# Row counts of a split DRAM write, and the place of a sign factor, in an FFT filter followed by a cosine-gated feed-forward

## The chip, the cores and the metric

The kernel runs on one core of a Trainium2 chip. The core has five engines that run side by side, each through its own list of instructions in order: TensorE (PE: matmuls; its weight loads are the separate row PEld), VectorE (DVE), ScalarE (ACT), GpSimd (POOL) and SyncE (SP), which here only issues DMA transfers. ScalarE issues transfers too. All transfers go through sixteen DMA engines. The metric is the device time of one execution in microseconds (us), the median of several runs.

## The reference

```python
def _attn_ref(x, filt_r, filt_i):            # x: (8, 3008, 256); filters: (1505, 256)
    X = np.fft.rfft(x, axis=1)
    F = (filt_r + 1j * filt_i)[None, :, :]
    return np.fft.irfft(X * F, n=x.shape[1], axis=1).astype(np.float32)

def _moe_ref(x, w_in, w_out):                # x: (24064, 256); w_in: (256, 2048); w_out: (2048, 256)
    h = x @ w_in
    g = h * np.cos(h)
    return (g @ w_out).astype(np.float32)
```

The second function is applied to the first one's result, with batch and sequence taken together. Everything is float32.

## The kernel before

**Arithmetic.** A float32 matmul of full accuracy is made of three faster ones: an operand is cut into a high part (a cast) and a low part (the rest), and `mm3` (L249) adds high x high, low matrix x high and high matrix x low. In the profile a cast to fp32r on ScalarE or VectorE is such a high part, and a TENSOR_TENSOR with subtraction, mostly on GpSimd, the low part.

**The filter** is a Fourier transform of length 3008 = 47 x 64 in four stages per batch. Stage 1 (L270) transforms over 47 and writes to DRAM (z1). `stage23` (L301) loads z1 in 12 pieces of 128 x 512 (zf), transforms over 64, multiplies by the filter, transforms back over 64 and writes to DRAM (z2). Stage 4 (L418) loads units of z2, transforms over 47 and makes the high and low part of y, the input of the feed-forward. A unit is up to five columns of the 64; there are 104, and the first three (5 + 5 + 1 columns, n_first = 3) feed the first chunk.

**The product with the filter** in `stage23`: the 128 rows of ps are 64 real parts and 64 imaginary parts. fat and fbt hold the filter's real and imaginary part, each twice, over the rows. ScalarE copies ps with its halves swapped into sw (L319, L320), VectorE multiplies ps by fat (L322), and sw by a sign per row and by fbt, in two halves of 256 columns, since each half has its own column of signs in sg (L325); then it adds the two (L327). sg holds minus the sign in its first 64 rows and plus the sign in the others. Before the next transform ScalarE makes the high part (L330) and GpSimd the low part (L331).

**The first batch** goes another way, at the start, with plain float32 matmuls: `first1` (stage 1), `first23` (L383; its z2t tiles are written to z2 here) and the first three units of stage 4. Each of the 12 tiles of `first23` has 128 rows: a column of the 64 has two of them. The write is cut in two after n0 rows: ScalarE's queue issues the first piece (L409), which the first three units need, and SP's queue the second (L412), later. n0 is 2 x 11 = 22, so the second piece has 106 rows of 2 KB.

**The feed-forward** has 47 chunks of 512 tokens, each in 8 steps: `hidden` (L458) makes a tile hp of 128 x 1024 in PSUM with 12 matmuls, `gate` (L473) makes g = h cos h with three VectorE steps (L476, L477, L479) and a Sin on ScalarE (L478) and cuts it into gh (L481, ScalarE) and gl (L483, GpSimd), and `project` (L486) adds it with 12 matmuls into two accumulators. There are two hp tiles; one is free again after L479. The weights w_in and w_out come as 64-bit floats in 16 tiles of 512 KB and are turned into high and low parts on the chip by `prep_w` (L214): the load (L222), two ScalarE steps (L231, L233), a shift on VectorE (L234), and GpSimd and ScalarE steps.

**Order.** The program fixes the order by a planner: `run_due` (L586) inserts the filter's steps for batches 1 to 7 and stage 4 between the matmuls of the feed-forward, by due times in slots. A scheduler that simulates the engines then sets the final order of each engine's list. On SP the beginning is written out by hand (L525 to L558): loads for the first batch, weights as listed in a string, then matrices. Transfers wait on eight shared completion counters, and each engine, SP too, stands at an instruction whose wait isn't over.

Of the kernel before, what the change touches and what calls it, by code (L numbers as in the profile page):

```python
# [13 lines left out]
AF = mybir.ActivationFunctionType  # L14
ALU = mybir.AluOpType

B, S, D, DFF = 8, 3008, 256, 2048
# [4 lines left out]
P = 128  # L22
# [116 lines left out]
def _units():  # L139


    sizes = [5, 5, 1] + [5] * 99 + [3, 3]
    assert sum(sizes) == B * NB
    starts = np.concatenate([[0], np.cumsum(sizes)])
    return [(int(a), int(n)) for a, n in zip(starts, sizes)]
# [10 lines left out]
def fft_filter_then_cos_glu(ctx: ExitStack, tc: tile.TileContext, ins, outT):  # L156
    nc = tc.nc
# [33 lines left out]
    sg = const.tile([P, NK], F32, name="sg")  # L191
# [6 lines left out]
    units = _units()  # L198
# [4 lines left out]
    n_first = len(of_chunk[0])  # L203

    @contextmanager
    def behind():

        if hold:
            with tc.issue_after(hold[0]):
                yield  # L210
        else:
            yield
# [36 lines left out]
    def mm3(out, m, hi, lo):  # L249

        nc.tensor.matmul(out, m[0], hi, start=True, stop=False)  # L251
        nc.tensor.matmul(out, m[1], hi, start=False, stop=False)  # L252
        nc.tensor.matmul(out, m[0], lo, start=False, stop=True)  # L253
# [7 lines left out]
    def psum_f(b):  # L261
        if b == 0 and len(done) < n_first:
            if not spare:
                spare.extend(ps_h.tile([P, 2, 512], F32, name="hp")[:, u] for u in range(2))
                spare.append(ps_f.tile([P, 512], F32, name="ps", tag="ps"))
            return spare.pop(0)
        return ps_f.tile([P, 512], F32, name="ps", tag="ps")
# [33 lines left out]
    def stage23(b, i):  # L301
        piece = slice(i * 512, (i + 1) * 512)
        f = fft.tile([P, 2, 512], F32, name="f", bufs=3)
        fbt, fat = f[:, 0], f[:, 1]
        with behind():
            nc.sync.dma_start(fbt, fb[:, piece])
            nc.sync.dma_start(fat, fa[:, piece])
        zf = fft.tile([P, 512], F32, name="zf", tag="ld", bufs=5)
        assert len(wrote1[b]) == 2 * n1
        nc.sync.dma_start(zf, z1s[b].rearrange("c (n k) d -> (c n) (k d)", k=NK)[:, piece])  # L310
        hi = fft.tile([P, 512], F32R, name="zh", tag="sh", bufs=3)
        lo = fft.tile([P, 512], F32R, name="zl", tag="sl", bufs=3)
        nc.vector.tensor_copy(hi, zf)  # L313
        nc.gpsimd.tensor_tensor(lo, zf, hi.bitcast(F32), ALU.subtract)  # L314
        yield
        ps = psum_f(b)
        mm3(ps, mats["m2"], hi, lo)
        sw = fft.tile([P, 512], F32, name="sw", bufs=2)
        nc.scalar.copy(sw[:64], ps[64:])  # L319
        nc.scalar.copy(sw[64:], ps[:64])  # L320
        ya = fft.tile([P, 512], F32, name="ya", bufs=2)
        nc.vector.tensor_tensor(ya, ps, fat, ALU.mult)  # L322
        for k in range(2):
            ks = slice(k * D, (k + 1) * D)
            nc.vector.scalar_tensor_tensor(sw[:, ks], sw[:, ks], sg[:, 2 * i + k : 2 * i + k + 1], fbt[:, ks],  # L325
                                           ALU.mult, ALU.mult)
        nc.vector.tensor_tensor(ya, ya, sw, ALU.add)  # L327
        yh = fft.tile([P, 512], F32R, name="yh", bufs=2)
        yl = fft.tile([P, 512], F32R, name="yl", bufs=2)
        nc.scalar.copy(yh, ya)  # L330
        nc.gpsimd.tensor_tensor(yl, ya, yh.bitcast(F32), ALU.subtract)  # L331
        yield
        ps = psum_f(b)
        if i == 0:
            mm3(ps[:, :D], mats["m30"], yh[:, :D], yl[:, :D])
            mm3(ps[:, D:], mats["m3"], yh[:, D:], yl[:, D:])
        else:
            mm3(ps, mats["m3"], yh, yl)
        z = fft.tile([P, 512], F32, name="z2t", tag="st", bufs=4)
        nc.scalar.copy(z, ps)  # L340
        wrote2.setdefault(b, []).append(i)
        nc.scalar.dma_start(z2[b * NJ : (b + 1) * NJ].rearrange("j (h c k) d -> (j h c) (k d)", h=2, c=2)[:, piece], z)
# [40 lines left out]
    def first23(i, fas, fbs):  # L383
        cols = slice(512 * i, 512 * i + 512)
        zf = fft.tile([P, 512], F32, name="zf", tag="ld", bufs=5)
        nc.sync.dma_start(zf, z1s[0].rearrange("j (h c k) d -> (j h c) (k d)", h=2, c=2)[:, cols])
        yield
        ps = psum_f(0)
        nc.tensor.matmul(ps, mats["f2"], zf, start=True, stop=True)
        half = slice(2 * (i % 2), 2 * (i % 2) + 2)  # L390
        ya = fft.tile([P, 512], F32, name="ya", bufs=2)
        yb = fft.tile([P, 512], F32, name="yb", tag="sw", bufs=2)
        for y, f in ((ya, fas), (yb, fbs)):
            nc.vector.tensor_tensor(y, ps, f[i // 2][:, half].rearrange("p k d -> p (k d)"), ALU.mult)
        yield
        ps = psum_f(0)
        if i == 0:
            for m, c in (("30", slice(0, D)), ("3", slice(D, 512))):
                nc.tensor.matmul(ps[:, c], mats["f" + m], ya[:, c], start=True, stop=False)
                nc.tensor.matmul(ps[:, c], mats["f" + m + "i"], yb[:, c], start=False, stop=True)  # L400
        else:
            nc.tensor.matmul(ps, mats["f3"], ya, start=True, stop=False)
            nc.tensor.matmul(ps, mats["f3i"], yb, start=False, stop=True)
        tag, bufs = at2[i]
        z = fft.tile([P, 512], F32, name="z2t", tag=tag, bufs=bufs)
        nc.scalar.copy(z, ps)
        to = z2[:NJ].rearrange("j (h c k) d -> (j h c) (k d)", h=2, c=2)[:, cols]
        n0 = 2 * units[n_first][0]
        nc.scalar.dma_start(to[:n0], z[:n0])  # L409
        yield  # L410
        wrote2.setdefault(0, []).append(i)
        nc.sync.dma_start(to[n0:], z[n0:])  # L412
# [112 lines left out]
    with tc.tile_pool(name="first", bufs=12) as first, tc.manual_schedule(engines={mybir.EngineType.SP}):  # L525
        fas, fbs, load, sign = filters(first)
        ones = [first1(i, first) for i in range(NJ // 4)]
        twos = [first23(i, fas, fbs) for i in range(n23)]
        for g in ones:
            next(g)  # L530
# [74 lines left out]
    for b in range(1, B):  # L605
        end = slot(b * S) - BEFORE
        if b == 1:
            end += LATER
        start = max(end - LENGTH, FIRST)
        step = (end - start - GAP12) / (2 * n1 + 2 * n23)  # L610
        for i in range(n1):
            t = start + step * (2 * i + 1)
            plan(stage1(b, i), t - AHEAD1, [t, t + step])
        for i in range(n23):
            t = start + step * (2 * n1 + 2 * i + 2) + GAP12
            plan(stage23(b, i), t - AHEAD2, [t, t + GAP23], lambda b=b: len(wrote1.get(b, ())) == 2 * n1)
# [73 lines left out]
```

## Time and profile before

| | |
|---|---|
| median of 3 runs | 2562.18 us (2557.64 to 2562.96) |
| the profiled execution | 2562.1 us |
| its span | 2560.3 us |
| mean granted TensorE clock | 0.979 |
| TensorE matmul busy | 2455.7 us (96%) |
| VectorE busy | 1885.4 us (74%) |
| ScalarE busy | 1286.1 us (50%) |
| GpSimd busy | 1430.5 us (56%) |
| DMA moved | 212.27 MB |
| TensorE idle, largest cause | 63.8 us in 15 waits for VectorE L479 |

Busy time is the time in which an engine has an instruction running. A share near 100% is a bound only in the stretch for which it is read: the table's 96% is a mean over a start in which TensorE often waits and a long rest. DMA-issuing instructions (SPq, ACTq) are not busy time; their length is the time that the issuing queue stood at them. "Granted clock" is the share of TensorE's full clock that the throttle let through.

### The profile page before, as it was taken

To read this page: it belongs to the slowest core of one execution; us is meant where nothing else is said; L and a number is where in the kernel's file an instruction comes from. 1 tells how busy PE (TensorE), PEld (TensorE's weight loads), DVE (VectorE), ACT (ScalarE), POOL (GpSimd) and SP (SyncE) were. 2 spreads that over 40 slices of the span, in tenths; PEclk is the share of its full clock that TensorE was granted. 3 is DMA by queue.
4 is the path that set the end of the run, shared out by engine and by line. 5 is a ranking of instruction groups with operands and counts; after the bars stand their busy time and mean duration, and the time that the engine had idled before them with its cause. 6 is when DMAs were issued, how large, how long until landed. Compare 5 with 4: busy or idle time off the path is not lost.

```text
span 2560.3 us, 29873 instructions
## 1 busy us (share of the span) xinstructions
PE 2455.7 (96%) x10783; PEld 1967.7 (77%) x10783; DVE 1885.4 (74%) x1911; ACT 1286.1 (50%) x1707; POOL 1430.5 (56%) x826
## 2 busy tenths in 40 slices
PE   7369889999999999999999999999999999999999
PEld 2257767888888888888888888888888888888887
DVE  2177987888678877888668886787768886666665
ACT  1355564555545555555545555455554554444443
POOL 1366664656656565656546665566555554444443
PEclk8679999999999999999999999999999999999999
DMA  9253342322322232222313223222312211000000
GB/s 318 72 166 89 129 144 65 119 82 82 85 83 91 90 91 71 93 90 78 93 47 105 86 85 85 79 94 74 100 43 88 99 54 48 24 21 9 17 9 17
DMA packets 134749, 212.27 MB, mean 83 GB/s; under 512 B 12521, under 2 KB 64281, under 8 KB 134601
## 3 DMA queue, kind: packets, MB, share of 16 engines
q1 hardware_dynamic: 82385, 137.97, 17.7%
q10 hardware_dynamic: 52216, 72.39, 8.8%
q8 instruction: 86, 1.41, 0.2%
q14 instruction: 62, 0.51, 0.1%
HBM read 135.33 MB, written 74.97 MB: 82 GB/s over the span
## 4 chain that ended last, share of the span: by engine, by line
PE 82%; DVE 7%; DMA 3%; issue 3%; SPq 2%; ACT 2%; POOL 1%; POOLq 0%; ACTq 0%; DVEq 0%
PE hp L466 36%; PE acc L495 36%; PE ps L435 3%; PE ps L251 2%; PE ps L252 2%; PE ps L253 2%; SPq L412 2%; DVE g L476 1%; DMA xf<-in_x 1%; DVE sw L325 1%; DVE g L477 1%; DMA raw<-in_w_in 1%; ACT g L478 1%; DVE g L479 1%; DVE xo L280 1%
## 5 line engine op out<-in xcount | busy, mean ns | idle before, releaser
L483 POOL TENSOR_TENSOR gl<-g,gh 128x1024 fp32r<-128x1024 f32 x376 | 910.7, 2422 | 825.6 <-ACT gh L481 510.7
L466 PE MATMUL hp<-y,w_in 128*128 128x512 f32 x4512 | 1132.6, 400 | 65.8 <-DVE g L479 63.8
L466 PEld LDWEIGHTS hp<-y,w_in 128*128 128x128 f32 x4512 | 845.3, 190 | 266.6 <-issue 59.8
L495 PE MATMUL acc<-gh,w_out 128*128 128x512 f32 x3008 | 896.9, 396 | 0.7 <-ACT gh L481 0.7
L479 DVE TENSOR_TENSOR g<-g,hp 128x1024 f32<-128x1024 f32 x376 | 457.9, 1218 | 320.6 <-ACT g L478 320.1
L478 ACT ACTIVATE g<-g,half_pi 128x1024 f32<-128x1024 f32 x376 | 433.4, 1153 | 484.2 <-DVE g L477 436.6
L495 PEld LDWEIGHTS acc<-gh,w_out 128*128 128x128 f32 x3008 | 564.0, 188 | 131.1 <-ACT gh L481 1.1
L481 ACT CAST gh<-g 128x1024 fp32r<-128x1024 f32 x376 | 394.9, 1051 | 430.5 <-DVE g L479 424.1
L476 DVE TENSOR_SCALAR g<-hp 128x1024 f32<-128x1024 f32 x376 | 458.8, 1220 | 137.7 <-PE hp L466 130.3
L495 PE MATMUL acc<-gl,w_out 128*128 128x512 f32 x1504 | 549.9, 400 | 1.3 <-POOL gl L483 1.3
L477 DVE SCALAR_TENSOR_TENSOR g<-g,hp 128x1024 f32<-128x1024 f32 x376 | 458.0, 1218 | 9.9
L495 PEld LDWEIGHTS acc<-gl,w_out 128*128 128x128 f32 x1504 | 283.7, 189 | 66.7 <-POOL gl L483 2.1
L452 POOL TENSOR_TENSOR y<-y,y 128x470 fp32r<-128x470 f32 (+29 forms) x142 | 124.9, 884 | 55.8 <-ACT y L449 55.8
L435 PEld LDWEIGHTS ps<-m,z 120*128 120x128 f32 (+1 forms) x816 | 129.3, 192 | 21.0
L314 POOL TENSOR_TENSOR zl<-zf,zh 128x512 fp32r<-128x512 f32 x84 | 111.7, 1330 | 47.8 <-DVE zh L313 24.5
L331 POOL TENSOR_TENSOR yl<-ya,yh 128x512 fp32r<-128x512 f32 x84 | 113.2, 1348 | 42.1 <-ACT yh L330 42.0
L435 PE MATMUL ps<-m,z 120*128 120x120 f32 (+1 forms) x816 | 129.2, 273 | 0.0
L325 DVE SCALAR_TENSOR_TENSOR sw<-sw,sg,f 128x256 f32<-128x256 f32 x168 | 116.9, 735 | 0.0
L313 DVE CAST zh<-zf 128x512 fp32r<-128x512 f32 x84 | 93.1, 1108 | 23.1 <-DMA zf<-z 13.4
L327 DVE TENSOR_TENSOR ya<-ya,sw 128x512 f32<-128x512 f32 x84 | 98.5, 1173 | 0.0
L330 ACT CAST yh<-ya 128x512 fp32r<-128x512 f32 x84 | 51.8, 618 | 91.0 <-DVE ya L327 90.7
L449 ACT CAST y<-y 128x470 fp32r<-128x470 f32 (+29 forms) x150 | 66.9, 456 | 41.3 <-DVE y L443 38.9
(96 smaller groups left out, 1413.3 us busy)
## 6 DMA issues: line engine op xcount, KB each, us to landing
z<-z SPq DMA_DIRECT2D x101, 240.0 KB
out_t<-o ACTq DMA_DIRECT2D x94, 256.0 KB
f<-in_fb SPq DMA_DIRECT2D x84, 256.0 KB
f<-in_fa SPq DMA_DIRECT2D x84, 256.0 KB
zf<-z SPq DMA_DIRECT2D x84, 256.0 KB
z<-z2t ACTq DMA_DIRECT2D x84, 256.0 KB
xf<-in_x SPq DMA_DIRECT2D x42, 480.0 KB
z<-z1t ACTq DMA_DIRECT2D x84, 240.0 KB
```

Source lines behind the costliest of these rows:

```text
L325: nc.vector.scalar_tensor_tensor(sw[:, ks], sw[:, ks], sg[:, 2 * i + k : 2 * i + k + 1], fbt[:, ks], ALU.mult, ALU.mult)
L331: nc.gpsimd.tensor_tensor(yl, ya, yh.bitcast(F32), ALU.subtract)
L435: nc.tensor.matmul(v[:, t, a * r : (a + 1) * r], zf[:, a, t * P : (t + 1) * P], mats[f"m4{a}"][:r, :r], start=True, stop=True)
L452: (nc.vector if i < 2 * n_first else nc.gpsimd).tensor_tensor(yl, part, yh.bitcast(F32), ALU.subtract)
L466: nc.tensor.matmul(hp[:, u], w_in[s][w][:, t, fs], y[:, t], start=(t == 0 and n == 0), stop=(t == NDT - 1 and n == 2))
L476: nc.vector.tensor_scalar(g, h, 0.25, MAGIC, ALU.add, ALU.add)
L477: nc.vector.scalar_tensor_tensor(g, g, MAGIC, h, ALU.subtract, ALU.subtract)
L478: nc.scalar.activation(g, g, AF.Sin, bias=half_pi, scale=-TWO_PI)
L479: nc.vector.tensor_tensor(g, g, h, ALU.mult)
L481: nc.scalar.copy(gh, g)
L483: nc.gpsimd.tensor_tensor(gl, g, gh.bitcast(F32), ALU.subtract)
L495: nc.tensor.matmul(acc, w_out[s][w][:, u, es], g[:, u], start=(s == 0 and u == 0 and n == 0), stop=(s == NFT // 2 - 1 and u == 1 and n == 2))
```

## The change

It does two things. In `first23` the write of a tile is cut after 32 rows instead of after 22: the first piece (ScalarE's queue) has 32 rows and the second (SP's queue) 96. The rows written, in sum, are the same. In `stage23` ScalarE's swapped copy becomes four activations of 64 x 256 (function Identity) that multiply by the sign as they copy, with the sign of the rows they read; VectorE then multiplies sw by fbt in one piece of 128 x 512 and subtracts where it added, since the rows read have the opposite sign of the rows written.

```diff
@@ -316,15 +316,14 @@
         ps = psum_f(b)
         mm3(ps, mats["m2"], hi, lo)
         sw = fft.tile([P, 512], F32, name="sw", bufs=2)
-        nc.scalar.copy(sw[:64], ps[64:])
-        nc.scalar.copy(sw[64:], ps[:64])
+        for k in range(2):
+            ks = slice(k * D, (k + 1) * D)
+            for to, of in ((slice(0, 64), slice(64, P)), (slice(64, P), slice(0, 64))):
+                nc.scalar.activation(sw[to, ks], ps[of, ks], AF.Identity, scale=sg[of, 2 * i + k : 2 * i + k + 1])
         ya = fft.tile([P, 512], F32, name="ya", bufs=2)
         nc.vector.tensor_tensor(ya, ps, fat, ALU.mult)
-        for k in range(2):
-            ks = slice(k * D, (k + 1) * D)
-            nc.vector.scalar_tensor_tensor(sw[:, ks], sw[:, ks], sg[:, 2 * i + k : 2 * i + k + 1], fbt[:, ks],
-                                           ALU.mult, ALU.mult)
-        nc.vector.tensor_tensor(ya, ya, sw, ALU.add)
+        nc.vector.tensor_tensor(sw, sw, fbt, ALU.mult)
+        nc.vector.tensor_tensor(ya, ya, sw, ALU.subtract)
         yh = fft.tile([P, 512], F32R, name="yh", bufs=2)
         yl = fft.tile([P, 512], F32R, name="yl", bufs=2)
         nc.scalar.copy(yh, ya)
@@ -405,7 +404,7 @@
         z = fft.tile([P, 512], F32, name="z2t", tag=tag, bufs=bufs)
         nc.scalar.copy(z, ps)
         to = z2[:NJ].rearrange("j (h c k) d -> (j h c) (k d)", h=2, c=2)[:, cols]
-        n0 = 2 * units[n_first][0]
+        n0 = 32
         nc.scalar.dma_start(to[:n0], z[:n0])
         yield
         wrote2.setdefault(0, []).append(i)
```

Lines from L327 of the old program on have numbers lower by one in the new one, so its second write is L411 and its load of a unit L424. The scheduler sets the lists of all engines anew. Two places of them:

SP's list, at the end of the twelve second pieces of the first batch's writes. z2t is the tile written, raw_684, raw_695 and raw_751 are the weights w_out, w_in and w_out of the fifth and sixth step, f the filter pieces of batch 1, z4_619 and z4_624 the loads of stage 4's units 3 and 4. Before:

```order
L412 DMA z2_112<-z2t_526 106x512
L222 DMA raw_684<-in_w_out 128x2x512
L306 DMA f_1529<-in_fb 128x512
L307 DMA f_1529<-in_fa 128x512
L306 DMA f_1593<-in_fb 128x512
L307 DMA f_1593<-in_fa 128x512
L306 DMA f_1648<-in_fb 128x512
L222 DMA raw_695<-in_w_in 128x2x512
L307 DMA f_1648<-in_fa 128x512
L222 DMA raw_751<-in_w_out 128x2x512
L425 DMA z4_619<-z2_112 120x2x256
L425 DMA z4_624<-z2_112 120x2x256
```

Here both units' loads stand behind the three weights and three pairs of filter pieces. SP's list at the same place, in the change:

```order
L411 DMA z2_112<-z2t_526 96x512
L424 DMA z4_619<-z2_112 120x2x256
L222 DMA raw_684<-in_w_out 128x2x512
L306 DMA f_1529<-in_fb 128x512
L307 DMA f_1529<-in_fa 128x512
L306 DMA f_1593<-in_fb 128x512
L307 DMA f_1593<-in_fa 128x512
L222 DMA raw_695<-in_w_in 128x2x512
L306 DMA f_1648<-in_fb 128x512
L222 DMA raw_751<-in_w_out 128x2x512
L424 DMA z4_624<-z2_112 120x2x256
```

Unit 3's load has moved up to stand right behind the writes, the second w_in (raw_695) has moved up by one, and one filter load (f_1648 of in_fa) has moved down behind what is shown.

TensorE's list, around the third hidden tile of the first chunk (hp_706). z4_619 and z4_624 are again units 3 and 4, y0 and y1 the high and low part of the first chunk, m40 and m41 stage 4's matrices. Before, the end of that tile:

```order
L466 MATMUL hp_706<-y0_554,w_in0_2_84 128x512
L466 MATMUL hp_706<-y1_555,w_in0_2_84 128x512
L466 MATMUL hp_706<-y0_554,w_in1_2_85 128x512
L435 MATMUL ps_621<-m40_310,z4_619 128x120
L435 MATMUL ps_621<-m41_312,z4_619 128x120
```

The two units' eight matmuls come after all twelve of the tile. TensorE's list in the change, the beginning of that tile:

```order
L434 MATMUL ps_657<-m41_312,z4_624 128x120
L434 MATMUL ps_657<-m40_310,z4_624 128x120
L465 MATMUL hp_706<-y0_554,w_in0_2_84 128x512
L465 MATMUL hp_706<-y1_555,w_in0_2_84 128x512
L465 MATMUL hp_706<-y0_554,w_in1_2_85 128x512
```

Unit 3's four matmuls and three of unit 4's now stand ahead of the tile.

## The prediction

> **What bounds the kernel now.** I read the waits of TensorE first, then its timeline, then followed the longest wait back through VectorE, ScalarE and SP's queue. A wait's row is engine, line, what it waited for: us in total, times, longest; a timeline row is start, length, instructions, and in brackets the idle time before it and its releaser.
>
> ```profile
> PE hp L466 <- DVE g L479: 63.8, 15, 48.2
> ...
> PE ps L251 <- DVE ya L322: 4.8, 3, 2.2
> ...
> PE hp L466 <- ACT y L449: 2.0, 1, 2.0
> ...
> PE acc L495 <- ACT gh L481: 0.7, 1, 0.7
> ...
> 400.00:2200.00 1800.00, 1798.65 (x8088) 1464.04 (x8087) 1401.64 (x1430) 955.52 (x1268) 1058.13 (x615) 1.00 0.26 81
> ```
>
> The last row is a window: its length, then busy time of PE, PEld, DVE, ACT and POOL, the granted clock, the DMA share and GB/s. From 400 us on TensorE never stands still, at a granted clock of 1.00; DVE is busy 78% there and ACT 53%. So an edit inside that stretch is worth nothing, and what is worth something is the first 400 us, where one single wait takes 48.2 us. Its chain, backwards:
>
> ```profile
> 143.80 4.58 PE L466 MATMUL hp<-y,w_in 128*128 128x512 f32 x12 [48.24 <-DVE g L479]
> ...
> 137.32 0.43 DVE L234 TENSOR_SCALAR t<-o 128x512 int32<-128x512 int32 x1 [46.97 <-ACT o L231]
> ...
> 136.55 0.66 ACT L231 ACTIVATE o<-raw 128x512 f32<-128x512 f32 x1 [44.14 <-DMA raw<-in_w_out]
> ...
> 122.52 4.30 SPq L222 DMA_DIRECT2D raw<-in_w_out  x1
> ...
> 79.06 43.36 SPq L412 DMA_DIRECT2D z<-z2t  x12
> ...
> 78.62 0.40 SPq L222 DMA_DIRECT2D raw<-in_w_in  x1
> ```
>
> TensorE wants a hidden tile back that VectorE frees (L479). VectorE stands in order behind L234, a step of the conversion of the fifth w_out tile; that waits for ScalarE, that for the raw weights, and their load was issued only at 122.52 because SP spent 43.36 us on the twelve writes of line 412. Those are slow in the engines that carry them:
>
> ```profile
> z<-z2t SPq DMA_DIRECT2D x12, 212.0 KB
> ...
> 84.00:126.00 42.00, 9.59 (x31) 7.41 (x30) 3.27 (x10) 4.58 (x10) 6.58 (x5) 0.58 0.13 51
> ...
> 1.19 11.82 SPq L373 DMA_DIRECT2D xf<-in_x  x16
> ...
> xf<-in_x SPq DMA_DIRECT2D x23, 192.0 KB
> ...
> 2.00:13.00 11.00, 9.03 (x14) 3.26 (x15) 1.67 (x3) 1.96 (x5) 0.00 (x0) 1.00 0.99 277
> ```
>
> While the 106-row writes run alone, the 16 DMA engines are busy 0.13 of the time at 51 GB/s: 0.13 x 16 is two engines. 217,088 bytes at 51 GB/s are 4.26 us each, 51 us for twelve. The 96-row loads of line 373 at the start (same row of 2 KB, 192 KB each) keep the share at 0.99 and move 277 GB/s; sixteen of them cost SP 11.82 us, 0.74 each.
>
> By the Trainium skill, page "DMA: Bandwidth & Descriptors", section "Why a DMA increments its semaphore by 16 and not by 1", a transfer uses the largest number of engines up to 16 that divides its slowest dimension. By that rule 106 rows get 2, 96 and 32 rows 16, and the 0.13 and the 0.99 agree with it. No row here is a 96-row write by itself; if the rule is taken to hold for writes too, the third rival below loses its chance of 0.05 to the forecast, whose time stays.
>
> **Part one, the first batch's writes.**
>
> ```profile
> L409 ACTq DMA_DIRECT2D z<-z2t x12: 287/288/537, 41.8 to 75.1; - x12
> ...
> z<-z2t ACTq DMA_DIRECT2D x12, 44.0 KB
> ...
> 76.63 1.28 SPq L425 DMA_DIRECT2D z<-z  x3
> ```
>
> SP's second pieces have 96 rows now, 196,608 bytes. Priced by line 373's rows, twelve take 12 x 0.74 = 8.9 us of SP where they took 43.36. ScalarE's twelve first pieces (L409) grow from 44 to 64 KB; 20 KB more at 277 GB/s are 0.07 us each, and they are issued between the weight conversions, up to 75 us. I cost them at nothing; if the last one landed later, the stage-4 loads at 76.63 would be late by that 0.07.
>
> In SP's list, shown above with the change, unit 3 (rows 22 to 31 of the tiles) now needs only the first pieces, so its load moved up past nine transfers; unit 4 still needs the twelve second pieces and follows the same loads as before. In TensorE's list the matmuls of both units moved ahead of the third hidden tile (hp_706), the one that stood 48 us.
>
> So TensorE restarts when two things are there, the freed hidden tile and unit 4's load, and I time both.
>
> ```profile
> f<-in_fb SPq DMA_DIRECT2D x84, 256.0 KB
> ...
> raw<-in_w_in SPq DMA_DIRECT2D x8, 512.0 KB
> ...
> z<-z SPq DMA_DIRECT2D x101, 240.0 KB
> ...
> 1.19 2.65 DMA xf<-in_x
> ...
> 141.74 10.22 DMA raw<-in_w_in
> ...
> 131.50:149.50 18.00, 5.70 (x24) 4.84 (x25) 8.59 (x10) 8.93 (x12) 6.56 (x5) 0.56 0.90 273
> ...
> 126.86 1.16 SPq L306 DMA_DIRECT2D f<-in_fb  x1
> ...
> 152.05 0.68 ACT L231 ACTIVATE o<-raw 128x512 f32<-128x512 f32 x1 [3.90 <-DMA raw<-in_w_in]
> ...
> 154.08 0.34 SPq L278 DMA_DIRECT2D xf<-in_x  x1
> ...
> 152.82 1.44 DVE L234 TENSOR_SCALAR t<-o 128x512 int32<-128x512 int32 x1 [2.43 <-POOL gl L483]
> ```
>
> *Hidden tile.* SP: 79.06 + 8.9 = 88.0, unit 3's load 0.4, so the weights go out at 88.4. From issue to use, 192 KB took 2.65 us on an empty queue; 320 KB more at 277 GB/s add 1.2, so 3.8 is the low end. The high end is 10.2, the weights at 141.74 behind a full queue. Ahead of ours stand only one 240 KB load and the rest of the writes, so I take 3.8: data at 92.2 instead of 136.55. From there to TensorE it was 143.80 - 136.55 = 7.25 us: 99.5 (up to 105.9).
>
> *Unit 4.* Behind raw_684 go five filter loads of 256 KB, two weights of 512 KB and unit 4's 240 KB, about 2.6 MB; at 273 GB/s, which the window around the same mix of transfers shows, 9.5 us from about 91 (the SP time for nine issues, at 0.4 to the 1.16 seen, lies inside it), plus about 1 us until its first three matmuls are through: 101.5. With the weights late by the 6.4 above it would be 108.
>
> The later one counts: 101.5 instead of 143.8, **42.3 us**, with 36 and 44.3 as ends.
>
> What is late next: the following weights landed at 151.96, 8.2 us after the restart, and ScalarE had waited 3.90 us for them and VectorE 2.43, partly because two of the sixteen engines were still draining the old writes. In the new order they go out right behind unit 4's group with an even queue, so I take the 2.4 of VectorE back; the ends are 0 and 3.9.
>
> **Part two, the filter product in batches 1 to 7** (84 pieces). What it removes and adds, by rows (line, engine, shape, count; busy, mean ns; idle before and why):
>
> ```profile
> L319 ACT COPY sw<-ps 64x512 f32<-64x512 f32 x84 | 49.1, 584 | 10.1 <-PE ps L253 8.3
> ...
> L320 ACT COPY sw<-ps 64x512 f32<-64x512 f32 x84 | 48.7, 579 | 1.0
> ...
> L295 ACT COPY z1t<-ps 96x256 f32<-96x256 f32 x14 | 4.9, 357 | 3.1 <-PE ps L253 3.1
> ...
> L478 ACT ACTIVATE g<-g,half_pi 128x1024 f32<-128x1024 f32 x376 | 433.4, 1153 | 484.2 <-DVE g L477 436.6 <-POOL gl L483 22.7 <-POOL yl L331 10.1
> ...
> L481 ACT CAST gh<-g 128x1024 fp32r<-128x1024 f32 x376 | 394.9, 1051 | 430.5 <-DVE g L479 424.1
> ...
> L325 DVE SCALAR_TENSOR_TENSOR sw<-sw,sg,f 128x256 f32<-128x256 f32 x168 | 116.9, 735 | 0.0
> ...
> L327 DVE TENSOR_TENSOR ya<-ya,sw 128x512 f32<-128x512 f32 x84 | 98.5, 1173 | 0.0
> ...
> 143.80:400.00 256.20, 234.10 (x993) 184.23 (x994) 217.79 (x219) 141.38 (x209) 173.46 (x104) 0.95 0.41 123
> ```
>
> VectorE: two products of 735 ns become one 128x512 product of two SBUF operands, for which L327 is the same form: 2 x 735 - 1173 = 0.30 us less per piece (nothing, if it were as slow as both old ones). ScalarE: two copies of 584 and 579 ns, together 1.16, become four activations of 256 columns. A plain copy of 256 columns took 357 ns; an activation with a vector operand took 1153 - 1051 = 102 ns more than a cast of the same shape. That gives 4 x 0.46 = 1.84, 0.68 us more; with no extra for the operand it is 0.27, with two such extras 1.08.
>
> The Trainium skill, page "ScalarE: Activation LUTs", section "What ACT_TABLE_LOAD costs", gives 186 ns plus 0.833 ns a column, and 93 ns for each vector operand. By it four pieces are about 1.97 us, an estimate, 0.8 more than the two copies' rows; the end at the loss side of this part, 8 us below, would be 12 x 0.8 = 9.6 by it, and the sum the same.
>
> Where does this lie? Batch 1's twelve pieces fall into the stretch up to 400 us, where VectorE is busy 218 of 256 us and a few short waits of TensorE depend on it (4.8 us for L322 in all); the other 72 lie under a full TensorE. So VectorE's gain is at most 12 x 0.30 = 3.6 us and ScalarE's longer step, if it delayed VectorE each time, at most 12 x 0.68 = 8.2 lost; the two go against each other with neither shown to be on the path each time, and I count **nothing**, from 4 gained to 8 lost. The cover in the later batches is ScalarE's slack (53% busy) and 0.7 us of waits for its gh; without it 72 x 0.68 = 49 us would appear.
>
> **Sum**, against the profiled execution, which took 2562.1 us with a span of 2560.3 (the median of the runs is 2562.18, so the same): 2562.1 - 42.3 - 2.4 + 0 = 2517.4, **2517 us**. The likeliest case alone runs from the ends 44.3 + 3.9 + 4 = 52 to 36 - 8 = 28 saved, which would need every end at once; 2509 to 2528 is what I hold for it.
>
> **Rivals.**
> 1. *The queue takes the wait over* (0.15). From 78.62 to unit 4's load 6.8 MB are issued (twelve writes and the loads counted above), 25 us at 273 GB/s; if weights, filters, unit 4 and stage 1's x all arrive at the late ends, 36 us are left and the 2.4 become a loss of about 3: 33 saved, 2529 us. For it: DMA share 0.90 already around 140 us. Against: the x loads came after 154 us.
> 2. *The short waits go too* (0.13). After the restart TensorE lost 15.6 us more to L479 (63.8 - 48.2) and 4.8 to L322, behind a VectorE filled with late weights. If half of it goes with the even queue and the lighter product, 44 + 10 = 54 us: 2508.
> 3. *It doesn't do what it says* (0.05): SP's time goes by rows, not by engines. Then 96 rows cost 43.36 x 96/106 = 39.3, 4.1 us saved: 2558. Line 373's 0.74 us speaks against it.
> 4. *Slower* (0.04): ScalarE's four pieces stand ahead of the Sin and the cast of a gate in its order; each late gate holds a hidden tile, and TensorE waits. It needs over 45 / 84 = 0.53 us of TensorE per piece in all seven batches to undo the gain; at 1.08 it would be 91 - 45 = 46 us slower, 2563 at the point of balance and 2608 at worst, 2580 in the middle. Against it: TensorE waited for ScalarE's y and gh 2.7 us in the whole run.
>
> The main case keeps 0.63. The range takes in rivals 1 and 2: **2505 to 2534**. A measurement of this kernel tells 0.2%, 5 us, from no change; faster 0.92 (the main case, rivals 1 and 2, and a bit of the other two), same 0.04, slower 0.04.
>
> **What would show it.** Right: line 411's twelve issues on SP take about 9 us; the fifth w_out weights reach ScalarE near 92 us; TensorE's wait of 48 us shrinks to about 6 and its releaser is L478 or unit 4's load; the DMA share around 85 us is near 1; the window from 400 us on is as full as before; the four activations take about 0.46 us each. Wrong: 3 us or more per write (rival 3), waits of TensorE for DMA between 100 and 150 us (rival 1), or waits for gh or L477 in the later batches (rival 4).

## The result, and the profile after

| | before | after |
|---|---|---|
| median | 2561.7 us | 2525.9 us |
| profiled execution, its span | 2562.1, 2560.3 us | 2526.6, 2524.8 us |
| restart of TensorE after the long wait | 143.80 us | 103.39 us |
| from there to the end of the span | 2416.5 us | 2421.4 us |
| VectorE, ScalarE busy | 1885.4, 1286.1 us | 1869.2, 1345.3 us |

The ratio of after to before is 0.9862 (95% interval 0.9845 to 0.9879), 36 us less. The forecast was 2517 us with a range of 2505 to 2534. The third and fourth rows already divide the result: the restart came 40.4 us earlier, and 4.9 us were lost again between the restart and the end. One of the six executions of part one alone, further down, took 4029 us at a granted clock of 0.56 and is left out of its ratio.

The timelines of SP, ScalarE and TensorE of the changed kernel, with the rows that answer to the chain shown of before (start, length, instructions; in brackets the idle time before and its releaser):

```profile
79.34 8.62 SPq L411 DMA_DIRECT2D z<-z2t  x12
88.79 0.79 SPq L222 DMA_DIRECT2D raw<-in_w_out  x1
94.45 2.32 SPq L424 DMA_DIRECT2D z<-z  x4
```

```profile
94.47 0.68 ACT L231 ACTIVATE o<-raw 128x512 f32<-128x512 f32 x1 [0.76 <-DMA raw<-in_w_out]
```

```profile
102.09 1.64 PE L434 MATMUL ps<-m,z 120*128 120x120 f32 x6 [4.01 <-DMA z<-z]
103.39 1.63 PE L465 MATMUL hp<-y,w_in 128*128 128x512 f32 x3
...
134.38 7.42 PE L465 MATMUL hp<-y,w_in 128*128 128x512 f32 x24 [2.06 <-DVE g L478]
...
153.32 7.95 PE L465 MATMUL hp<-y,w_in 128*128 128x512 f32 x21 [4.55 <-DVE g L478]
```

The twelve writes take SP 8.62 us instead of 43.36, the fifth w_out weights reach ScalarE at 94.47 instead of 136.55, and the wait of 48.24 us is gone; in its place TensorE waits 4.01 us for unit 4's load. But further on stand waits of 2.06 and 4.55 us; the longest in this stretch before was 2.3 us. The waits of TensorE of the changed kernel, from its restart on (engine, line, what it waited for: us in total, times, longest):

```profile
PE hp L465 <- DVE g L478: 20.3, 17, 4.6
PE acc L494 <- ACT gh L480: 2.7, 4, 1.4
PE acc L494 <- POOL gl L482: 2.6, 2, 1.3
PE ps L251 <- ACT z1t L295: 1.6, 2, 0.9
```

Before, the same stretch had 15.6 us of waits for L479 beside the long one, 4.8 for L322, 3.1 for L443 and 2.0 for gh and gl: 25.5 us. Now these rows and three small ones hold 28.4.

Part two by itself, in the rows that group the changed kernel's instructions:

```profile
L322 ACT ACTIVATE sw<-ps,sg 64x256 f32<-64x256 f32 x336 | 157.9, 470 | 13.0 <-PE ps L253 6.9 <-PE acc L494 0.4 <-ACT z2t L339 0.4
L326 DVE TENSOR_TENSOR ya<-ya,sw 128x512 f32<-128x512 f32 x84 | 102.2, 1217 | 0.4
L325 DVE TENSOR_TENSOR sw<-sw,f 128x512 f32<-128x512 f32 x84 | 93.9, 1117 | 0.0
L324 DVE TENSOR_TENSOR ya<-ps,f 128x512 f32<-128x512 f32 x84 | 57.8, 688 | 45.0 <-ACT sw L322 44.3 <-POOL zl L314 0.6
```

The four activations take 4 x 470 = 1.88 us, against 1.16 for the two copies. VectorE's product takes 1117 ns against 1470, and the subtraction 1217 against 1173: 0.31 us less per piece. VectorE now stands 44.3 us in front of L324 until ScalarE's fourth piece is done, where it stood 9.6 before; whether that reaches TensorE the experiments had to tell.

### The profile page after: what moved, and what is told of

It reads as the page before. It is cut to its first block, busy times and chain, and to the rows that moved or that the text cites. A ratio compares the mean times of both kernels' runs of the same rounds, so it can differ in the third digit from the quotient of the medians.

```text
span 2524.8 us, 29967 instructions
## 1 busy us (share of the span) xinstructions
PE 2459.7 (97%) x10783; PEld 1969.5 (78%) x10783; DVE 1869.2 (74%) x1827; ACT 1345.3 (53%) x1875; POOL 1424.2 (56%) x826
## 4 chain that ended last, share of the span: by engine, by line
PE 81%; DVE 8%; DMA 4%; ACT 3%; issue 2%; POOL 1%; SPq 0%; POOLq 0%; ACTq 0%; DVEq 0%
PE hp L465 37%; PE acc L494 35%; PE ps L434 3%; PE ps L251 2%; PE ps L253 2%; PE ps L252 2%; DMA xf<-in_x 2%; DVE g L476 1%; DVE g L475 1%; DVE g L478 1%; ACT sw L322 1%; ACT g L477 1%; DVE ya L326 1%; DVE sw L325 1%; DVE xo L280 1%
## 5 line engine op out<-in xcount | busy, mean ns | idle before, releaser
L465 PE MATMUL hp<-y,w_in 128*128 128x512 f32 x4512 | 1135.3, 400 | 23.8 <-DVE g L478 20.3
L478 DVE TENSOR_TENSOR g<-g,hp 128x1024 f32<-128x1024 f32 x376 | 457.8, 1218 | 309.0 <-ACT g L477 308.5
L475 DVE TENSOR_SCALAR g<-hp 128x1024 f32<-128x1024 f32 x376 | 458.4, 1219 | 119.3 <-PE hp L465 114.2
L476 DVE SCALAR_TENSOR_TENSOR g<-g,hp 128x1024 f32<-128x1024 f32 x376 | 457.9, 1218 | 9.6
L322 ACT ACTIVATE sw<-ps,sg 64x256 f32<-64x256 f32 x336 | 157.9, 470 | 13.0 <-PE ps L253 6.9
L313 DVE CAST zh<-zf 128x512 fp32r<-128x512 f32 x84 | 93.6, 1114 | 22.7 <-DMA zf<-z 20.3
L326 DVE TENSOR_TENSOR ya<-ya,sw 128x512 f32<-128x512 f32 x84 | 102.2, 1217 | 0.4
L280 DVE TENSOR_TENSOR xo<-xf 120x512 f32<-120x512 f32 (+1 forms) x49 | 52.6, 1075 | 58.2 <-DMA xf<-in_x 58.1
```

Of the source, the lines that this page charges most:

```text
L322: nc.scalar.activation(sw[to, ks], ps[of, ks], AF.Identity, scale=sg[of, 2 * i + k : 2 * i + k + 1])
L326: nc.vector.tensor_tensor(ya, ya, sw, ALU.subtract)
L465: nc.tensor.matmul(hp[:, u], w_in[s][w][:, t, fs], y[:, t], start=(t == 0 and n == 0), stop=(t == NDT - 1 and n == 2))
L475: nc.vector.tensor_scalar(g, h, 0.25, MAGIC, ALU.add, ALU.add)
L476: nc.vector.scalar_tensor_tensor(g, g, MAGIC, h, ALU.subtract, ALU.subtract)
L478: nc.vector.tensor_tensor(g, g, h, ALU.mult)
```

## The experiments

Two questions: whether the gain of part one is the number of DMA engines that carry a piece, and where the 4.9 us after the restart went.

**Part one alone.** Edit to the kernel before:

```diff
-        n0 = 2 * units[n_first][0]
+        n0 = 32
```

> Part one alone (rows 32 and 96, the old filter product). Theory A, that part one brings what the restart gained (143.80 to 103.39 us) and that part two costs about 5 us later, under TensorE's full stretch: about 2520 us, with TensorE's idle from 400 to 2200 us back at 1 to 2 us and L322 waiting for ScalarE's copies about 8 us as before. Theory B, that part two is neutral and the missing 5 us come with part one (the shift of the feed-forward against the other batches, or the new order): 2525 us, the same as the whole change within its interval.

Measured: 2517.8 us, ratio 0.9834 (0.9821 to 0.9847). That is 8 us less than the whole change, so within these lists part two cost something. TensorE's idle between 400 and 2200 us was 2.9 us, against 8.1 in the whole change, which is the direction that theory A gave. Its restart came at 102.25 us, behind unit 4's load as in the whole change:

```profile
100.95 1.63 PE L435 MATMUL ps<-m,z 120*128 120x120 f32 x6 [5.27 <-DMA z<-z]
102.25 1.20 PE L466 MATMUL hp<-y,w_in 128*128 128x512 f32 x2
```

From there to the end of its span of 2515.5 us it took 2413.3 us, 3.3 less than the kernel before.

**Part two alone.** Edit to the kernel before: the filter product as in the change, with n0 left at 22.

```diff
-        nc.scalar.copy(sw[:64], ps[64:])
-        nc.scalar.copy(sw[64:], ps[:64])
...
+                nc.scalar.activation(sw[to, ks], ps[of, ks], AF.Identity, scale=sg[of, 2 * i + k : 2 * i + k + 1])
...
+        nc.vector.tensor_tensor(sw, sw, fbt, ALU.mult)
+        nc.vector.tensor_tensor(ya, ya, sw, ALU.subtract)
```

> Part two alone (rows 22 and 106, the new product). Theory A: 5 us slower than before, 2566 to 2568 us, with TensorE idle 7 to 9 us between 400 and 2200 us. Theory B: no change, 2559 to 2564 us. The forecast of this part was from 4 us gained to 8 lost.

Measured: 2551.0 us, ratio 0.9962 (0.995 to 0.9974): 9.4 us *faster*, which neither theory had. Part two gains 9 us on the old writes and loses 8 on the new. Both theories fall in this form, and a new one was needed that explains both signs.

The lists gave it. The scheduler simulates the engines and sets their order anew for every edit. TensorE's list has 10,313 matmuls. Compared place by place, by operands without their buffer numbers, part two has another matmul than the kernel before in 7,173 places, part one (with unit 3's load set free) in 5,243, and the whole change differs from part one alone in 7,031. Most of these only moved along with others; 900 to 1,000 matmuls of each pair really stand in another order. So each of these runs compares two kernels in two orders. Cuts after 24, 27 or 30 rows, where unit 3 still needs the second pieces, leave TensorE's and VectorE's lists exactly as before, and these separate the speed of a write from the order.

**Cut after 27 rows.** Edit to the kernel before:

```diff
-        n0 = 2 * units[n_first][0]
+        n0 = 27
```

> The old product, and the write cut after 27 rows, so that SP's pieces have 101 rows, 5 fewer than before. If the piece's number of engines is the largest divisor of its rows up to 16, 101 rows use one engine: 206848 bytes at half of 51 GB/s are 8.1 us each, twelve 97 us on SP, and the kernel takes about 2610 us. If SP's time goes by rows or bytes, twelve take 41 us and the kernel 2560 us.

Measured, one run with a profile: 2605.5 us. SP's timeline and a window of it (length, granted clock, DMA share, GB/s):

```profile
79.10 85.50 SPq L412 DMA_DIRECT2D z<-z2t  x12
```

```profile
90.00:170.00 80.00, 0.54 0.07 26
```

Five rows fewer per piece, and the twelve issues took twice as long: 85.5 us at 26 GB/s and a share of 0.07, one engine of sixteen. TensorE's long wait was 94.80 us. Time by rows or bytes is excluded.

**Cut after 24 rows.** The same edit with n0 = 24.

> The old product, and the write cut after 24 rows: SP's pieces have 104 rows, 2 fewer than before, and unit 3 still waits for them. By divisors 104 rows use eight engines, 204 GB/s: about 1.05 us each, 12.5 on SP, and the kernel takes about 2530 us. By rows or bytes: 42.5 us on SP, 2561 us. If the gain came from unit 3's load that no longer waits for the second pieces, and not from the speed of the pieces, 2560 us too.

Measured, one run with a profile: 2519.9 us, and the twelve issues took 9.98 us. Its window while the writes run:

```profile
86.00:88.00 2.00, 0.50 0.85 325
```

The divisor theory holds, but the expectation applied it wrongly: the largest divisor of 104 up to 16 is 13, not 8. Thirteen engines are a share of 0.81, and 0.85 was seen. Two rows fewer than 106 cut the long wait to 7.56 us, in exactly the old order of TensorE's work, with unit 3 still behind the second pieces:

```profile
102.71 5.46 PE L466 MATMUL hp<-y,w_in 128*128 128x512 f32 x12 [7.56 <-DVE g L479]
```

So the speed of the writes is the gain, not unit 3's freed load.

**Cut after 30 rows, old product.** The same edit with n0 = 30.

> The old product and a cut after 30 rows (98 rows on SP, fourteen engines by divisors). Every engine's list is that of the kernel before, apart from a few rows around the writes' first pieces, and unit 3 still waits for the second pieces: the speed of the writes alone. Theory A and B: 2519 to 2522 us, like the cut after 24.

Measured: 2517.1 us, ratio 0.9827 (0.9813 to 0.984), a little less than expected; the window from 86 to 88 us has a share of 0.93 (fourteen engines: 0.88).

**Cut after 30 rows, new product.** Edit to the changed kernel:

```diff
-        n0 = 32
+        n0 = 30
```

> The new product and a cut after 30 rows: the lists are those of part two alone, in which unit 3's load stays behind. Theory A, that part two is worth 9 us in that list and that the whole change loses it again through its other list, with unit 3 ahead: 2509 to 2513 us. Theory B, that part two gains only where the long wait gives the other engines time, and costs wherever the start is quick: 2524 to 2528 us.

Measured: 2508.9 us, ratio 0.9797 (0.9783 to 0.981). Theory A held, at the edge of its range. With TensorE's list of part two alone, the gains add: 42.9 for the writes, and 8.2 more for part two (9.4 with the slow writes). This version beats both kernels, the changed one by 17 us, and it differs from that one in two rows of the cut and in the list. The two rows hardly tell: the twelve issues took SP 8.62 us there and 9.20 here. TensorE's two lists differ in 917 of the 10,313 places, none behind place 1,251. The waits of this version after its restart at 103.04 us:

```profile
PE hp L465 <- DVE g L478: 8.0, 11, 1.4
PE ps L251 <- ACT z1t L295: 3.0, 2, 2.1
PE acc L494 <- POOL gl L482: 2.8, 2, 1.5
PE ps L251 <- DVE y L442: 2.3, 1, 2.3
```

8.0 us for L478 instead of 20.3, none above 1.4. And VectorE's wait for ScalarE's sw is the same as in the whole change, row for row:

```profile
L324 DVE TENSOR_TENSOR ya<-ps,f 128x512 f32<-128x512 f32 x84 | 57.8, 688 | 44.7 <-ACT sw L322 44.3 <-issue 0.2
```

So the 44.3 us that VectorE stands in front of L324 aren't what the whole change lost against this version. Where the longest of its waits behind the restart comes from can be seen in VectorE's timeline of the changed kernel ahead of the 4.55 us wait:

```profile
137.10 2.25 DVE L281 TENSOR_TENSOR xf<-xf 120x512 f32<-120x512 f32 x1
139.27 4.60 DVE L280 TENSOR_TENSOR xo<-xf 120x512 f32<-120x512 f32 x2
143.79 3.48 DVE L281 TENSOR_TENSOR xf<-xf 120x512 f32<-120x512 f32 x2
147.19 1.21 DVE L475 TENSOR_SCALAR g<-hp 128x1024 f32<-128x1024 f32 x1
```

Five steps of batch 1's stage 1 stand in a row, 10 us, and the gate that would free a hidden tile (L475, L476, L478) comes behind them; TensorE ran out of work at 148.8 and restarted at 153.3.

Most of the 17 us went later, though. TensorE's matmul records can be counted off in both traces (10,783 in each, more than the list has matmuls, since a plain float32 one leaves two). The 501st starts at 192 us in the changed kernel, 2.9 us later than in this version; the 1,367th, from which on the two lists are the same, at 404 us, 13.8 later; the last one 16.7 later. The largest single piece, some 6 us, lies between 380 and 400 us, here of the changed kernel, VectorE and then TensorE:

```profile
376.98 1.12 DVE L280 TENSOR_TENSOR xo<-xf 120x512 f32<-120x512 f32 x1 [1.97 <-DMA xf<-in_x]
378.02 1.21 DVE L476 SCALAR_TENSOR_TENSOR g<-g,hp 128x1024 f32<-128x1024 f32 x1
...
380.51 1.22 DVE L478 TENSOR_TENSOR g<-g,hp 128x1024 f32<-128x1024 f32 x1 [0.68 <-ACT g L477]
```

```profile
382.92 1.20 PE L494 MATMUL acc<-gh,w_out 128*128 128x512 f32 x4 [1.44 <-ACT gh L480]
385.42 0.79 PE L494 MATMUL acc<-gl,w_out 128*128 128x512 f32 x1 [1.30 <-POOL gl L482]
```

VectorE stands in order at a step of stage 1 whose x hasn't landed, the gate's steps come behind it, and TensorE waits for what the gate makes, gh and gl. From 384.8 to 391.6 its granted clock was then 0.50. From the restart to the end the changed kernel waited 28.4 us and this version 18.1. The rest is the clock, in these windows of the changed kernel and then of this version (length, busy times of PE, PEld, DVE, ACT, POOL, clock, DMA share, GB/s):

```profile
103.00:200.00 97.00, 89.97 (x372) 71.95 (x372) 84.30 (x73) 51.90 (x78) 70.76 (x42) 0.92 0.37 103
200.00:400.00 200.00, 188.47 (x811) 148.10 (x810) 155.43 (x154) 115.38 (x176) 122.16 (x74) 0.98 0.37 113
```

```profile
103.00:200.00 97.00, 90.86 (x390) 72.19 (x391) 80.26 (x80) 54.96 (x84) 73.37 (x43) 0.96 0.43 116
200.00:400.00 200.00, 193.28 (x854) 154.24 (x853) 159.43 (x161) 120.86 (x184) 124.80 (x76) 0.99 0.39 116
```

0.04 of 97 us and 0.01 of 200 are about 6 us, an estimate. With the 10.3 us of waits that makes 16 of the 16.7 us between the two, so the difference is short waits and the clock behind them.

**Two other lists, old product.** Edits to the cut after 30 rows with the old product, one number of the planner each:

```diff
-LATER = 54
+LATER = 53
```

> The cut after 30 rows with the old product, and one number of the planner changed (LATER 53 for 54): the same instructions, in lists that differ in half of TensorE's rows from batch 1 on. Theory A says that a list alone is worth several us: some 3 to 10 us away from the cut after 30 rows, either way. Theory B says that it is the product: within 2 us of it.

```diff
-FIRST, LENGTH, BEFORE = 60, 376, 160
+FIRST, LENGTH, BEFORE = 61, 376, 160
```

> The same with another number of the planner (FIRST 61 for 60), LATER at 54 again. Theory A: 3 to 10 us away from the cut after 30 rows, either way. Theory B: within 2 us.

Measured: 2525.9 us, ratio 0.9864 (0.9851 to 0.9878), and 2511.9 us, ratio 0.981 (0.9796 to 0.9823). The same instructions with the same writes, 8.8 us slower and 5.2 us faster than 2517.1: theory A again. A list alone is worth that.

**The same two lists' numbers, new product.** The same two edits to the cut after 30 rows with the new product, FIRST 61 first.

> The new product, the cut after 30 rows, FIRST 61: the partner of the old product with FIRST 61 (2511.9 us). If the lighter VectorE product itself is worth the 8 us between the two runs with FIRST 60 (2517.1 and 2508.9), this gives 2503 to 2506 us. If those 8 us are the list's, as the 8 us lost in the whole change are, the difference may have either sign: 2505 to 2522 us, and the sign here tells nothing more than that.

> The same with LATER 53 and FIRST 60; its partner with the old product took 2525.9 us. If the product itself is worth 8 us: 2517 to 2519 us. If the list decides: anywhere in 2508 to 2530 us.

Measured: 2518.9 us, ratio 0.9846 (0.9831 to 0.986), and 2510.2 us, ratio 0.9813 (0.9797 to 0.983). All pairs, old product against new:

| start and planner | old, us | new, us | new - old |
|---|---|---|---|
| cut 22 (slow writes) | 2560.4 | 2551.0 | -9.4 |
| cut 32 (unit 3 early) | 2517.8 | 2525.9 | +8.1 |
| cut 30 | 2517.1 | 2508.9 | -8.2 |
| cut 30, FIRST 61 | 2511.9 | 2518.9 | +7.0 |
| cut 30, LATER 53 | 2525.9 | 2510.2 | -15.7 |

The first and the third pair have the same two TensorE lists and agree within 1.2 us, so the number is steady for a list. Over lists the sign changes, as the two last expectations gave it for the case that the list decides. The four quick pairs have a mean of -2.2 us and run from -15.7 to +8.1. That is no wider than lists alone would make it: the old product's four quick times lie within 14 us, the new product's within 17. Nor are the new product's lists four independent ones. That of LATER 53 differs from that of the plain cut after 30 rows in 22 places (2510.2 and 2508.9 us), that of FIRST 61 from the changed kernel's in 324 (2518.9 and 2525.9). And the kernel before, measured again beside each group of runs, had medians from 2559.1 to 2561.7 us, so some 2 us of each difference mean nothing. Part two's own worth therefore can't be told from these runs. What stays open is whether it is a few us for better, for worse, or nothing; a test would need both products in one fixed list, and that wasn't tried, since the scheduler makes a new list for every product.

## Why the prediction was right or wrong

**Part one was right in its mechanism and nearly in its size.** Two engines for 106 rows, read from the share of 0.13, was confirmed by four other row counts (0.07 for 101, 0.85 for 104, 0.93 for 98, and about 1.05 for 96). SP's 8.9 us were 8.62. The weights' arrival at 92.2 was 94.47: the low end of 3.8 us from issue to use was 5.7, while the DMA engines were still full (a share of 0.99 from 88 to 90 us). Unit 4, the later of the two conditions, was forecast to decide, and did in this list; 101.5 was 103.39. (In the old list, cut after 24 rows, it was the hidden tile, at 102.71.) So 42.3 us were 40.4. Rival 3 (time by rows) is out.

**The step that failed is part two's "nothing".** I took 2.4 us back after the restart ("what is late next") and counted part two as zero; instead the stretch from the restart to the end grew by 4.9 us. 1.9 us from the restart and 7.3 from there on make up the 9.2 between 2517.4 and the profiled 2526.6. Part one alone tells the two terms apart: there the stretch behind the restart was 3.3 us shorter, and in the old list 1.7 and 1.1 (cuts after 30 and 24 rows). So the 2.4 were about right. With part two added to part one the restart came 1.1 us later and the rest took 8.2 us more. The term wasn't mis-sized but missing: I had looked at the two changed places of the lists for the restart only, and priced part two by its instructions (+0.68 us on ScalarE and -0.30 on VectorE for each piece, measured +0.72 and -0.31) as if the rest of the order stayed. It didn't; in 7,658 of its 10,313 places TensorE's list had another matmul than before, and that was there to be read. An order of the same work costs from 2511.9 to 2525.9 us here, more than either of my bounds on part two.

**What was luck.** The 2525.9 lies in my range, and even in the 2509 to 2528 of the main case, because that had room for a loss of 8 us in part two. But that room was for ScalarE's longer step holding up VectorE in batch 1, and the version that is 17 us faster has the same longer step. And the 2517.2 of part one's profiled execution agree with my 2517.4 better than they should, since another order of the same work would have moved them by several us.

**Rival 1** (the queue takes the wait over) was right in 4 us, the wait for unit 4's load, which I had in the sum. Later there was no long wait of TensorE for DMA. (Its 6.8 MB were added up wrongly: the transfers it names are 6.3, 23 us instead of 25.) **Rival 2** (the short waits go too) did not happen in the change but did in the cut after 30 rows with the new product: 18 us of waits after the restart instead of 25.5, and 2508.9 us, close to its 2508. The nearness is luck in part: waits fell by 7 us there, not 10, and the clock gave the rest. Its condition was not the even queue that I named, which the changed kernel has too, but the list. **Rival 4** (ScalarE's four pieces hold up the gates) is not what cost those 17 us: TensorE's waits for gh rose only from 0.7 to 2.7 us, the longest of them behind a late gate on VectorE, and with the same four pieces and the same 44.3 us of waits at L324 the other list is 17 us faster.

**The full stretch.** The window that was to be as full as before was not quite:

```profile
400.00:2200.00 1800.00, 1791.91 (x8045) 1456.61 (x8044) 1386.38 (x1359) 1001.97 (x1403) 1049.96 (x611) 1.00 0.27 81
```

TensorE idled 8.1 us there where it idled 1.4 before, mostly waiting for L478. (The columns are those of the prediction's window rows.) The cut after 30 rows starts as early and idles 1.4 with the old product and 3.6 with the new one, so the earlier start doesn't explain the 8.1. But a list doesn't fix the number either: part two alone, in the same TensorE list as the 3.6, idles 7.3 there with its late start. How much of the 8.1 is the list stays open.

## What to carry to other kernels

A transfer's number of rows can matter more than its bytes: check the DMA share while a transfer runs alone, and if it is a small fraction of sixteen, cut the rows so that both pieces divide well (here 22 and 106 rows cost some 40 us that 24 and 104 did not). Where a scheduler or planner sets the order, an edit is a new order as well; a difference of a few us says something about the edit only if the order stayed the same, so look for a variant that changes the suspected cost and leaves the lists alone, or take several lists. And a stage bound by one engine is worth reading behind the first wait that is removed: the cluster of five steps in front of a gate was in the list, to be seen before any run, though not its 10 us.

## What the runs showed of the hardware

That the engines of a transfer follow the divisors of its rows was expected after the 0.13; that three rows fewer can change its rate from 325 to 26 GB/s (104 and 101 rows) had not been seen in this kernel.

Some short waits of TensorE cost more than their length. In the changed kernel the three stretches behind waits of 4.01, 2.06 and 4.55 us ran at a low granted clock (length, busy times of PE, PEld, DVE, ACT, POOL, clock, DMA share, GB/s):

```profile
103.40:110.30 6.90, 6.90 (x26) 5.71 (x26) 5.57 (x7) 5.00 (x9) 6.54 (x4) 0.65 1.02 309
134.40:141.60 7.20, 7.20 (x24) 5.74 (x25) 7.20 (x4) 4.64 (x8) 6.28 (x4) 0.76 0.52 142
153.30:161.30 8.00, 7.98 (x22) 6.32 (x23) 7.82 (x4) 3.30 (x5) 6.86 (x3) 0.61 0.30 86
```

At 0.61 to 0.76 of the clock these 22 us would have needed about 15 at full clock (6.9 x 0.65 + 7.2 x 0.76 + 8.0 x 0.61 = 14.8), so the three waits of 10.6 us cost some 7 us more, an estimate. Not every short wait does: behind one of 1.76 us in the changed kernel twelve matmuls took the usual 3.03 us, behind one of 1.99 us in the kernel before they took 4.59 (the changed kernel first):

```profile
285.94 3.03 PE L465 MATMUL hp<-y,w_in 128*128 128x512 f32 x12 [1.76 <-DVE g L478]
```

```profile
167.49 4.59 PE L466 MATMUL hp<-y,w_in 128*128 128x512 f32 x12 [1.99 <-DVE g L479]
```

The Trainium skill, page "TensorE: Matmul & The Clock Gate", section "Part 1: The HAM clock gate (the "warmup" mystery)", says that the clock falls to half after an idle window of about 3.4 us. The 4.01 and 4.55 us agree with it; after the 2.06 us, and in the kernel before after the 1.99 us, matmuls were slow too, so here shorter idle times were enough.
